# Token loads in pairs, query weights on ScalarE's queue, and two blocks' statistics moved, in the opening of a transformer layer on one core

## The chip, the cores and the metric

The kernel runs on one core of a Trainium2 chip. The metric is the device time of one execution in microseconds (us), as the median of several runs. A profiled execution gives the trace from which durations come; its span runs from its first to its last instruction.

The engines go by these names in the views: PE is TensorE's matmul and PEld its weight load, DVE is VectorE, ACT is ScalarE, POOL is GpSimd, SP is SyncE, which here only issues DMA transfers. Each engine runs its own instructions in order and waits for others on semaphores.

## The reference

One layer over 2048 tokens of width 640, in bf16: layer norm, attention with a compressive memory over four segments of 512 tokens and 32 heads of 20, a residual, a second layer norm, and a two-layer block with 1728 hidden units. Cut to what bears on the opening:

```
q = (layernorm(x) @ wq)   k = (layernorm(x) @ wk)   v = (layernorm(x) @ wv)
for s in range(4):
    p = softmax(qs @ ks^T * scale + mask)
    o = g * (phi(qs) @ M / (phi(qs) @ z)) + (1 - g) * (p @ vs)
    M += phi(ks)^T @ vs;  z += sum(phi(ks))
h  = x + o @ wo
h2 = h + silu(layernorm(h) @ w1) @ w2
```

The layer norm needs, for each token, mean and variance over 640 elements, and then `(x - mean) * (var + eps) ** -0.5`.

## The kernel before

Tokens are handled in blocks of 128 (one token per partition), four blocks to a segment; the block index is b. Weights stay in SBUF. The program is a graph of named tasks, and a hand-kept list, `ORDER` (L382), says in which order the tasks are emitted. Each engine's instruction stream is that list filtered for the engine; a suffix picks the engine where a task may run on two (`/D` VectorE, `/A` ScalarE, `/G` GpSimd), and numbers after a colon are buffer slots. A tracker turns reads and writes into semaphore waits, so a task waits only where it stands in its own engine's stream; what is behind it on that engine waits too.

The steps of the opening, for the first segment:

- `load_x` (L595, issued in L598) loads token blocks. Before, block 0 (`x0`), block 1 (`x1`) and blocks 2 and 3 together (`x2`) are three loads on SyncE.
- `load_w` (L600, issued in L601) loads weights. The query and key weights come in two pieces each (`w_q0`, `w_q1`, `w_k0`, `w_k1`: 3 and 2 of the 5 chunks of 128 rows) into the raw buffer `wraw`, then the value weights (`w_wv`) and `beta`. All are on SyncE, in this order. Blocks 4 to 11 (`x4`, `x8`) follow; they wait for the first piece of the key weights.
- `zpad` (L616) is a block of zeros made by VectorE. `warm` (L618) is one ScalarE activation of Tanh on it, whose output is overwritten later; a load of the activation table goes with it.
- `fillN` are N matmuls of zeros on TensorE (L637), which compute nothing.
- `n1_st` is a block's statistics. On VectorE (L785 to L791): two half-row statistics, their merge and, for the blocks called early, the addition of eps. On ScalarE (L778, L780): two activations with a running sum, which give the sum and the variance, and later `n1_mn` (L801), which gives the mean. Before, blocks 0, 1 and 3 are on VectorE and block 2 is on ScalarE.
- `n1_rs` is the reciprocal root on GpSimd: one power (L808) for early blocks, an addition and a power (L811, L813) for the others.
- `n1_ap` (L819) on VectorE applies mean and root. `n1_tp` (L828) transposes a block on TensorE by five matmuls with the identity, and `n1_te` copies the result out of PSUM, on ScalarE (L837) or VectorE (L838).
- `pr00` are the first projections, from the raw weights (L752): x and y are the first and the second half of the segment's tokens (blocks 0 and 1, blocks 2 and 3), the digit before them is 0 for queries and 1 for keys, and .0 and .1 are the two pieces of the weights. There are 80 matmuls in all. `re_wq` and `re_wk` (L745, L747) reorder the weights for the later projections.
- `mq0` and `mq1` (L703) are small masks on GpSimd, needed much later.

The order of the opening before (buffer slots left out), as far as the prediction walks it:

```
VectorE: zpad sel st0 st1 ap0 st3 ap1 ap3 ap2 te3 ...
ScalarE: warm st2 te0 mn2 te1 re_wq1 te2 ...
TensorE: fill25 fill4 fill8 tp0 tp1 fill2 tp3 pr000x.0 tp2 pr000x.1 pr001x.0 pr001x.1 pr001y pr000y ...
```

Of the kernel before, what the change touches and what calls it, by code (L numbers as in the profile page):

```python
# [11 lines left out]
PE, AC, DV, PO, SP = "pe", "act", "dve", "pool", "sp"  # L12
# [333 lines left out]
D = 640  # L346
# [26 lines left out]
KS = [range(0, 3), range(3, 5)]  # L373
# [7 lines left out]

ORDER = """  # L382
x0:0 zpad:0 iota fill25:7 vpad0 x1:3 sel halfc mq0 x2:5,6 warm:0 w_q0:0 epsc w_q1 n1_st0:1 w_k0:0 w_k1 w_wv:0 n1_st1:0
n1_rs0 beta n1_ap0:0 n1_rs1 fill4:5 n1_st2:5,1 n1_st3:4 fill8:5 mq1 n1_tp0:2 n1_ap1:2 n1_rs3 n1_te0:1 n1_tp1:0 n1_rs2
fill2:5 n1_ap3:3 n1_mn2 n1_te1 n1_tp3:6 n1_ap2 re_wq1/A:0 pr000x.0:3 n1_te3/D x4:2,10,11,1 n1_tp2:4 pr000x.1
x8:9,8,4,7 n1_te2 pr001x.0:1 qe000x/D:0 re_wk1/G pr001x.1 re_wk2/A pr001y.0:2 re_wk4/G pr001y.1 qe001x pr000y.0:6
qe001y pr000y.1 re_wk3/G pr010.0/C:0 pa001:2 qe000y ex001:1 re_wq2/G qk0a0:4,1 lsc0 pr010.1 e0a2:0 lsc1 pr011.0:7
qe010/D:0 e0a0 pr011.1 qk0b0:0,2 qe011/D pr020.0/C:6 e0b2:3 mk0a pb001 pr020.1/C re_wk0/G n1_st4:3 e0b0 qk0e0:2,4
pr021.0:7 re_wq4/G e0e0:5 n1_st5:1 v00.0:0 vpad2 n1_rs4 e0e2 v00.1 qe020/D:0 pr021.1 n1_rs5 n1_st10:7 ve00:0 qk1a0:2,4
# [94 lines left out]
def build(nc, es, A_x, A_wq, A_wk, A_wv, A_wo, A_beta, B_x, B_w1, B_w2, out):  # L484
    T = Tracker()
# [9 lines left out]
    G = Graph(pools)  # L495
# [7 lines left out]
    wv_sb = sb("wv_sb", [128, NC, D], BF16)  # L503
# [65 lines left out]
    def R(*items):  # L569
        r = []  # L570
        for a, subs in items:
            r += a.keys(subs)
        return r

    def dma(name, reads, writes, fn, prio, bw, kind="plain", lane=None, engs=(SP,)):
        ln = T.lane(name) if lane is None else lane

        def emit(eng):
            T.add(eng, lambda e: fn(e), reads=R(*reads), writes=R(*writes), lane=ln)
        cost = {"tr": 1.31, "plain": 0.47, "sb": 0.72, "fix": 0.47}[kind]  # L580
        t = G.task(name, {e: cost for e in engs}, emit, reads, writes, prio, mode=kind, bw=bw)
        return t
# [5 lines left out]
    W = {k: G.alloc(k) for k in ("wq", "wk", "wv", "wo", "w1", "w2")}  # L588
    C = G.alloc("const")
# [3 lines left out]
    sT0 = G.alloc("sT")  # L593

    def load_x(b0, n, prio, bw=2.1, kind="plain", engs=(SP, AC)):  # L595
        s0 = b0 % 12
        dma(f"x{b0}", [(W["wk"], ["p"])] if b0 >= 4 else [], [(X[b], [0]) for b in range(b0, b0 + n)],
            lambda e: e.dma_start(out=x_tok[:, s0:s0 + n, :], in_=xv[:, b0:b0 + n, :]), prio, bw, kind, engs=engs)  # L598

    def load_w(k, dst, src, prio, bw, wr, kind="plain", engs=(SP, AC)):  # L600
        dma("w_" + k, [(W["wk"], ["p"])] if kind == "plain" else [], wr, lambda e: e.dma_start(out=dst, in_=src), prio, bw, kind, engs=engs)  # L601

    cw = lambda w: w.rearrange("(c p) e -> p c e", p=128)
    load_x(0, 1, -100, 2.30, "fix", (SP,))
    load_x(1, 1, -99, 2.33, "fix", (SP,))
    load_w("wv", wv_sb[:, :, :], cw(A_wv), -98, 4.96, [(W["wv"], [0])], "fix", (SP,))
    load_x(2, 2, -97, 4.79, "fix", (SP,))
    dma("beta", [], [(C, ["beta_bc"])],
        lambda e: e.dma_start(out=beta_bc[:, :],
                              in_=A_beta.rearrange("(o n) -> o n", o=1).to_broadcast([128, H])), -92, 4.65, "fix")  # L610
    for w_, (n_, src) in enumerate((("q", A_wq), ("k", A_wk))):
        for z, ks in enumerate(KS):
            k0_, k1_ = ks[0], ks[-1] + 1
            load_w(f"{n_}{z}", wraw[:, w_, k0_:k1_, :], cw(src)[:, k0_:k1_, :], -94 + w_, 6.58, [(sT0, [f"{n_}{z}"])] + ([(W["wk"], ["p"])] if n_ + str(z) == "k0" else []), "fix",
                   (SP,))
    G.task("zpad", {DV: 0.3}, lambda e_: T.add(DV, lambda e: e.memset(zpad[:, :], 0.0), writes=R((C, ["zpad"]))),  # L616
           [], [(C, ["zpad"])], -101)
    G.task("warm", {AC: 1.15}, lambda e_: T.add(AC, lambda e: e.activation(  # L618
        out=w2_sb[:, NF - 1:NF + 1, :], in_=zpad[:, 0:1].unsqueeze(2).to_broadcast([128, 2, D]), func=ACT.Tanh),
        reads=R((C, ["zpad"])), writes=R((W["w2"], [4, 5]))), [(C, ["zpad"])], [(W["w2"], [4, 5])], -100)  # L620
# [28 lines left out]
    def vpad(par, vt, wr=()):  # L649
# [8 lines left out]
        writes=["iota"], prio=-70)  # L658
    cst("sel", DV, 0.12, lambda e: e.tensor_scalar(out=ident[:, :], in0=iot[:, :], scalar1=0.0, scalar2=None,
                                                   op0=ALU.is_equal), reads=["iota"], writes=["sel"], prio=-70)  # L660
    sel = ident[:, :].rearrange("p (r e) -> p r e", e=32)[:, :, 0:VS]
# [5 lines left out]
        out=bsel[:, :], in_=bsel[:, :], pattern=[[0, NG], [-32, 4]], compare_op=ALU.is_equal, fill=0.0, base=-DH,  # L667
        channel_multiplier=1), reads=["bsel"], writes=["bsel"], prio=-1)
    cst("lsc2", DV, 0.25, lambda e: e.tensor_reduce(
        out=lsc[:, :], in_=bsel[:, :].rearrange("p (g r) -> p g r", r=4), axis=mybir.AxisListType.X, op=ALU.add),  # L670
# [95 lines left out]
    def layer_norm(tag, b, xa, xsub, dstA, i, prio):  # L766
# [5 lines left out]
        def e_stats(eng):  # L772
# [17 lines left out]
            if early:  # L790
                T.add(DV, lambda e: e.tensor_scalar(out=mvt[:, s, 1:2], in0=mvt[:, s, 1:2], scalar1=EPS, scalar2=None,  # L791
                                                    op0=ALU.add),
                      reads=R((st, ["mv"])), writes=R((st, ["mv"])))
        early = tag == "n1_" and b in (0, 1, 3)
        onact = tag == "n1_" and b == 2
        G.task(f"{tag}st{b}", {AC: 1.6} if onact else {DV: 1.03}, e_stats, [(xa, xsub)],
               [(st, ["s0", "mv"] if onact else ["s0", "s1", "mv"])] + ([(xn, [0])] if onact else []), prio)
        if onact:
# [55 lines left out]
    def declare_front(s):  # L854
# [5 lines left out]
        for i in range(4):  # L860
            layer_norm("n1_", 4 * s + i, X[4 * s + i], [0], xTa, i, k0 + P["ln1"] + P["ln1s"] * i if s else -30 + i)
# [531 lines left out]
```

## Time and profile before

| | us |
|---|---|
| median of 3 runs | 292.81 (292.77 to 293.06) |
| the profiled execution | 292.8 |
| its span | 291.1 |

The profile's page gives, for each engine, its busy time and its share of the span. The chain of waits is followed back from the last instruction: each piece is the work, or the transfer, that the next piece waited for. The timeline lists instructions in order of time, with start and duration in us, neighbours of one kind merged, and in brackets how long the engine had been idle before them and who ended that. A table by stretches of time gives each engine's busy time, then the granted TensorE clock (PEclk), the mean busy share of the 16 DMA engines, and the GB/s that they moved. The list of DMA issues gives, for each kind of load, how many there were, the size of one and the median time from its issue to its landing, when the last byte is there and its waiter may go on.

### The profile page before, as it was taken

The numbers are of one execution on the slowest core, as the hardware profiler recorded it, in microseconds if no ns is written. First come the engines' busy times: TensorE is split into PE (matmuls) and PEld (weight loads), VectorE is DVE, ScalarE is ACT, GpSimd is POOL, SyncE is SP. The second block draws the span as 40 slices with busy tenths as digits, with TensorE's granted clock in tenths as the row PEclk, the third lists the DMA queues.
The fourth block names the chain that finished last, engine by engine and source line by source line (L and its number), as shares of the span: only waits on it lengthen the run. The fifth ranks groups of instructions, "written<-read, shape, count | busy, mean of one in ns | idle before, by whom it ended". The sixth has DMA issues, their size and how long they took to land.

```text
span 291.1 us, 10526 instructions
## 1 busy us (share of the span) xinstructions
PE 283.0 (97%) x4587; PEld 156.9 (54%) x4587; DVE 208.7 (72%) x435; ACT 224.7 (77%) x286; POOL 138.1 (47%) x275
## 2 busy tenths in 40 slices
PE   8999989999999999999999999999999999999995
PEld 6544434445544446566643554655565557754674
DVE  5599889769998679369979972776676659436513
ACT  4999999999999999999689989999849750024300
POOL 4686668608670766609516761638435531200000
PEclk9999999999999999999999999999999999999999
DMA  7916439854565333343551327512110031340004
GB/s 207 350 57 125 85 65 303 116 55 79 121 110 126 67 86 101 47 76 60 101 183 17 66 43 102 78 19 49 25 25 2 2 69 26 75 131 0 3 5 160
DMA packets 48734, 24.86 MB, mean 85 GB/s; under 512 B 38896, under 2 KB 47472, under 8 KB 48688
## 3 DMA queue, kind: packets, MB, share of 16 engines
q1 hardware_dynamic: 48688, 24.19, 37.9%
q8 instruction: 36, 0.59, 0.9%
q14 instruction: 10, 0.08, 0.1%
HBM read 10.41 MB, written 2.62 MB: 45 GB/s over the span
## 4 chain that ended last, share of the span: by engine, by line
PE 79%; ACT 13%; DVE 4%; DMA 2%; POOL 1%; issue 1%; SPq 0%; DVEq 0%; ACTq 0%
PE ps_all L565 41%; PE ps_all L566 23%; ACT PT L1024 9%; PE ps_all L1003 7%; PE ps_all L1059 5%; ACT PT L1020 2%; DMA x_tok<-in_A_x_dram 2%; PE ps_all L1130 1%; PE ps_all L752 1%; PE ps_all L1268 1%; ACT ex L930 1%; POOL PT L1036 1%; DVE om L1149 1%; ACT oTs L1073 1%; PE ps_all L1189 1%
## 5 line engine op out<-in xcount | busy, mean ns | idle before, releaser
L1024 ACT ACTIVATE PT<-ps_all 128x1024 bf16<-128x1024 f32 x122 | 117.9, 1030 | 7.9 <-PE ps_all L1003 6.8
L1036 POOL TENSOR_SCALAR_AFFINE_SELECT PT<-PT 128x512 bf16<-128x512 bf16 x128 | 81.6, 666 | 71.6 <-ACT PT L1024 59.5
L1281 ACT ACTIVATE th<-ps_all 128x512 f32<-128x512 f32 (+1 forms) x56 | 31.5, 591 | 30.1 <-PE ps_all L565 22.5
L1287 DVE SCALAR_TENSOR_TENSOR sT<-th,ps_all 128x512 bf16<-128x512 f32 (+1 forms) x56 | 36.2, 661 | 16.8 <-ACT th L1281 16.5
L1020 ACT ACTIVATE PT<-ps_all 128x2048 bf16<-128x2048 f32 x19 | 35.7, 1878 | 3.5 <-PE ps_all L1003 3.4
L565 PE MATMUL ps_all<-w_sb,sT 128*128 128x320 bf16 x252 | 37.0, 299 | 0.0
L565 PE MATMUL ps_all<-tT,w_sb 128*128 128x512 bf16 x151 | 36.4, 380 | 0.0
L1324 DVE SCALAR_TENSOR_TENSOR x_tok<-ps_all,x_tok 128x640 bf16<-128x640 f32 (+1 forms) x17 | 13.2, 782 | 24.5 <-PE ps_all L566 16.1
L565 PEld LDWEIGHTS ps_all<-w_sb,sT 128*128 128x128 bf16 x252 | 23.7, 98 | 11.0 <-issue 1.7
L566 PE MATMUL ps_all<-w_sb,sT 128*32 128x320 bf16 x784 | 28.8, 299 | 0.0
L785 DVE BATCH_NORM_STATS2 stt<-x_tok 128x6 f32<-128x320 bf16 x62 | 27.0, 478 | 2.0 <-DMA x_tok<-in_A_x_dram 1.9
L566 PE MATMUL ps_all<-tT,w_sb 128*32 128x512 bf16 x436 | 27.1, 380 | 0.0
L566 PEld LDWEIGHTS ps_all<-w_sb,sT 128*32 128x32 bf16 x784 | 20.1, 97 | 6.7 <-issue 0.9
L565 PEld LDWEIGHTS ps_all<-tT,w_sb 128*128 128x128 bf16 x151 | 13.6, 98 | 16.1 <-issue 1.9
L1111 POOL TENSOR_TENSOR otok<-otok,om 128x320 bf16<-128x320 bf16 x24 | 18.2, 781 | 4.2 <-DVE otok L1098 4.2
L565 PE MATMUL ps_all<-wv_sb,tT 128*128 128x320 bf16 x130 | 19.9, 300 | 0.2 <-DVE zf L677 0.2
L811 POOL TENSOR_TENSOR rst<-mvt,eps_c 128x1 f32<-128x1 f32 x29 | 5.8, 201 | 27.4 <-DVE mvt L788 27.4
L819 DVE TENSOR_SCALAR xn_rot<-x_tok,mvt,rst 128x640 bf16<-128x640 bf16 x32 | 16.7, 533 | 2.5 <-POOL rst L813 1.3
L813 POOL TENSOR_TENSOR rst<-rst,eps_c 128x1 f32<-128x1 f32 x29 | 16.4, 567 | 2.3
L1246 DVE TENSOR_TENSOR x_tok<-ps_all,x_tok 128x640 bf16<-128x640 f32 x16 | 13.0, 812 | 6.0 <-PE ps_all L565 6.0
L1059 PE MATMUL ps_all<-PT,Vx 128*32 128x512 bf16 (+3 forms) x384 | 16.9, 300 | 0.2 <-ACT PT L1024 0.2
L1098 DVE TENSOR_TENSOR otok<-ps_all,rd 128x320 bf16<-128x320 f32 x32 | 15.7, 491 | 1.1
(116 smaller groups left out, 427.8 us busy)
## 6 DMA issues: line engine op xcount, KB each, us to landing
out_dram<-x_tok SPq DMA_DIRECT2D x15, 160.0 KB, 2.0
w_sb<-in_B_w_dram SPq DMA_DIRECT2D x5, 432.0 KB, 4.6
x_tok<-in_A_x_dram SPq DMA_DIRECT2D x3, 640.0 KB, 5.1
w_sb<-in_B_w_dram SPq DMA_DIRECT2D x3, 480.0 KB, 4.1
QKV<-QK SPq DMA_DIRECT2D x12, 72.0 KB
wv_sb<-in_A_wv_dram SPq DMA_DIRECT2D x1, 800.0 KB, 8.9
wo_sb<-in_A_wo_dram SPq DMA_DIRECT2D x1, 800.0 KB, 4.8
w_sb<-in_B_w_dram SPq DMA_DIRECT2D x1, 640.0 KB, 4.7
```

The source lines that it names most:

```text
L565: return [lambda e: e.matmul(out, lhsT=lhsT, rhs=rhs, start=start, stop=stop)]
L566: return [lambda e, p=p: e.matmul(out[p:p + 32, :], lhsT=lhsT[:, p:p + 32], rhs=rhs, start=start, stop=stop, tile_position=(0, p)) for p i ...
L785: T.add(DV, lambda e, hh=hh: e.bn_stats(out=stt[:, s, 6 * hh:6 * hh + 6], in_=xb[:, 320 * hh:320 * hh + 320]), reads=R((xa, xsub)), writes ...
L819: T.add(eng, lambda e: e.tensor_scalar(out=xn_rot[:, xn.slot, :], in0=x_tok[:, b % 12, :], scalar1=mvt[:, s, 0:1], scalar2=rst[:, s, :], o ...
L1003: fns.append(lambda e, j=j, o=o, r=r, q0=q0, q1=q1, qa=qa, ka=ka: e.matmul(ps_all[:, o:o + q1 - q0], lhsT=ka[32 * r:32 * r + DH, 128 * j:1 ...
L1020: T.add(AC, lambda e: e.activation(out=o, in_=src, func=ACT.Exp, scale=SCALE), reads=[("ps", z.slot + q) for z in (a, b) for q in range(2) ...
L1024: T.add(AC, lambda e: e.activation(out=pt[:, pta.slot, q0:q0 + 2, 0:width], in_=sc3[:, b0:b0 + 2, 0:width], func=ACT.Exp, scale=SCALE), re ...
L1036: fns.append(lambda e, v=v: e.affine_select(out=v, in_=v, pattern=[[0, 4], [1, 128]], compare_op=ALU.is_ge, fill=0.0, base=0, channel_mult ...
L1059: fns.append(lambda e, j=j, r=r, h=h, pa=pa, pt=pt, co=co, q0=q0, ji=ji: e.matmul(bank(po)[32 * r:32 * r + 32, q0:hi], lhsT=vtile(vx)[:, j ...
L1111: T.add(PO, lambda e: e.tensor_tensor(out=o_dst, in0=o_dst, in1=m, op=ALU.add), reads=R((oma, WH), *osub), writes=R(*osub))
L1281: T.add(AC, lambda e: e.activation(out=th[:, tha.slot, lo:hi], in_=bank(ps)[:, lo:hi], func=ACT.Tanh, scale=0.5), reads=R((ps, [0])), writ ...
L1287: T.add(DV, lambda e: e.scalar_tensor_tensor(out=sT[:, f, lo:hi], in0=th[:, tha.slot, lo:hi], scalar=1.0, in1=bank(ps)[:, lo:hi], op0=ALU. ...
```

## The change

Four things change; all of them lie in the first row of `ORDER` and the declarations behind it.

1. Blocks 0 and 1 are one load (`x0`), as blocks 2 and 3 are. SyncE issues `x0`, `x2`, `w_k0`, `w_k1`, `w_wv`, `beta`, in this order.
2. `w_q0` and `w_q1` are issued by ScalarE. They are declared as reading `zpad`, so the first of them waits for the zero block. They stand ahead of `warm` on ScalarE.
3. The statistics of blocks 1 and 3 are on ScalarE, and those of block 2 on VectorE. Accordingly the early blocks, with one power on GpSimd, are 0 and 2, and there are `mn1` and `mn3` on ScalarE in place of `mn2`.
4. The first row of the order is rewritten up to `pr001x.0`, and is the old one from there on. On VectorE: st0 st2 ap0 ap1 ap2 te0 ap3 te3. On ScalarE: w_q0 w_q1 warm st1 mn1 st3 mn3 te1 te2 re_wq1. On GpSimd: rs0 rs1 mq1 rs2 rs3. On TensorE: fill25 fill4 tp0 fill8 tp1 tp2 fill2 pr000x.0 pr000x.1 tp3 pr001x.0. The copy of block 0 out of PSUM goes from ScalarE to VectorE.

```diff
 ORDER = """
-x0:0 zpad:0 iota fill25:7 vpad0 x1:3 sel halfc mq0 x2:5,6 warm:0 w_q0:0 epsc w_q1 n1_st0:1 w_k0:0 w_k1 w_wv:0 n1_st1:0
-n1_rs0 beta n1_ap0:0 n1_rs1 fill4:5 n1_st2:5,1 n1_st3:4 fill8:5 mq1 n1_tp0:2 n1_ap1:2 n1_rs3 n1_te0:1 n1_tp1:0 n1_rs2
-fill2:5 n1_ap3:3 n1_mn2 n1_te1 n1_tp3:6 n1_ap2 re_wq1/A:0 pr000x.0:3 n1_te3/D x4:2,10,11,1 n1_tp2:4 pr000x.1
-x8:9,8,4,7 n1_te2 pr001x.0:1 qe000x/D:0 re_wk1/G pr001x.1 re_wk2/A pr001y.0:2 re_wk4/G pr001y.1 qe001x pr000y.0:6
+x0:0,3 zpad:0 iota w_q0:0 w_q1 fill25:7 vpad0 sel halfc mq0 x2:5,6 warm:0 epsc w_k0:0 w_k1 w_wv:0 beta n1_st0:1 n1_st1:0,2 n1_rs0 n1_st2:5 fill4:5 n1_ap0:0 n1_rs1 mq1 n1_mn1 n1_tp0:2 n1_ap1 fill8:5 n1_tp1:0 n1_rs2 n1_st3:4,3 n1_ap2:1 n1_mn3 n1_rs3 n1_te0/D:1 n1_te1/A n1_tp2:4 n1_ap3 n1_te2 fill2:5 pr000x.0:3 pr000x.1 re_wq1/A:0 n1_tp3:6 n1_te3/D x4:2,10,11,1 x8:9,8,4,7 pr001x.0:1 qe000x/D:0 re_wk1/G pr001x.1 re_wk2/A pr001y.0:2 re_wk4/G pr001y.1 qe001x pr000y.0:6
...
-    load_x(0, 1, -100, 2.30, "fix", (SP,))
-    load_x(1, 1, -99, 2.33, "fix", (SP,))
-    load_w("wv", wv_sb[:, :, :], cw(A_wv), -98, 4.96, [(W["wv"], [0])], "fix", (SP,))
-    load_x(2, 2, -97, 4.79, "fix", (SP,))
...
+    load_x(0, 2, -100, 2.80, "fix", (SP,))
+    load_x(2, 2, -97, 3.40, "fix", (SP,))
+    for w_, (n_, src) in enumerate((("q", A_wq), ("k", A_wk))):
+        for z, ks in enumerate(KS):
+            k0_, k1_ = ks[0], ks[-1] + 1
+            dma(f"w_{n_}{z}", [(C, ["zpad"])] * (n_ == "q"), [(sT0, [f"{n_}{z}"])] + [(W["wk"], ["p"])] * (n_ + str(z) == "k0"),
+                lambda e, w_=w_, k0_=k0_, k1_=k1_, src=src: e.dma_start(out=wraw[:, w_, k0_:k1_, :], in_=cw(src)[:, k0_:k1_, :]),
+                -94 + w_, 5, "fix", engs=((AC, SP)[w_],))
+    load_w("wv", wv_sb[:, :, :], cw(A_wv), -90, 4.96, [(W["wv"], [0])], "fix", (SP,))
...
-        early = tag == "n1_" and b in (0, 1, 3)
-        onact = tag == "n1_" and b == 2
+        early = tag == "n1_" and b in (0, 2)
+        onact = tag == "n1_" and b in (1, 3)
```

The numbers in these declarations (priorities and costs) are not used when the order is written out by hand.

More of the change, by code (lines that the diff above doesn't have):

```diff
@@ L603, in build @@
     cw = lambda w: w.rearrange("(c p) e -> p c e", p=128)
-    load_x(0, 1, -100, 2.30, "fix", (SP,))
-    load_x(1, 1, -99, 2.33, "fix", (SP,))
-    load_w("wv", wv_sb[:, :, :], cw(A_wv), -98, 4.96, [(W["wv"], [0])], "fix", (SP,))
-    load_x(2, 2, -97, 4.79, "fix", (SP,))
+    G.task("zpad", {DV: 0.3}, lambda e_: T.add(DV, lambda e: e.memset(zpad[:, :], 0.0), writes=R((C, ["zpad"]))),
+           [], [(C, ["zpad"])], -101)
+    load_x(0, 2, -100, 2.80, "fix", (SP,))
[7 more added lines that the diff above has]
+    load_w("wv", wv_sb[:, :, :], cw(A_wv), -90, 4.96, [(W["wv"], [0])], "fix", (SP,))
     dma("beta", [], [(C, ["beta_bc"])],
@@ L610, in build @@
                               in_=A_beta.rearrange("(o n) -> o n", o=1).to_broadcast([128, H])), -92, 4.65, "fix")
[L611 to L617, printed above, removed]
     G.task("warm", {AC: 1.15}, lambda e_: T.add(AC, lambda e: e.activation(
```

## The prediction

> **What bounds the kernel now.** I read the page first, for what fills the span, and then the chain of waits in the first 14 us, because the diff touches only the loads and the first row of the written order.
>
> ```profile
> span 291.1 us, 10526 instructions
> PE 283.0 (97%) x4587; PEld 156.9 (54%) x4587; DVE 208.7 (72%) x435; ACT 224.7 (77%) x286; POOL 138.1 (47%) x275
> PE 79%; ACT 13%; DVE 4%; DMA 2%; POOL 1%; issue 1%; SPq 0%; DVEq 0%; ACTq 0%
> ```
>
> TensorE is busy all through, and the chain that ended last is TensorE with some ScalarE. So what the opening gains or loses should reach the end nearly whole: nothing behind it has room to give it back. The opening itself, from the chain restricted to 0 to 14 us (start, us, what):
>
> ```profile
> 1.72 4.91 DMA x_tok<-in_A_x_dram
> ...
> 6.65 0.90 DVE stt L785 x2
> 7.57 0.22 DVE mvt L788
> 7.82 0.16 DVE mvt L791
> 8.06 0.69 POOL rst L808
> 8.85 0.46 DVE xn_rot L819
> ...
> 9.80 0.47 PE ps_all L752 x12
> 10.31 0.45 PE ps_all L828 x5
> 10.77 2.07 PE ps_all L752 x68
> ```
>
> The reader sees that blocks 2 and 3 of the tokens, one load issued at 1.72, land at 6.63, and that statistics, root, apply, transposes and first projections (L752) follow without a gap. The opening is a race between the landing of blocks 2 and 3 and the steps behind it. The mark I use is the start of the second token half's projections (pr001y), when block 2 has been copied out of PSUM:
>
> ```profile
> 11.56 0.99 PEld L752 LDWEIGHTS ps_all<-tT,sT 128*32 128x32 bf16 x40 [0.20 <-ACT tT L837]
> ```
>
> From that task on the written order is the old one, so the change of the whole time is the change of this 11.56.
>
> **When the tokens land.** Issues and landings by load, and what the DMA moved (last column GB/s):
>
> ```profile
> x_tok<-in_A_x_dram SPq DMA_DIRECT2D x2, 160.0 KB, 2.3
> x_tok<-in_A_x_dram SPq DMA_DIRECT2D x1, 320.0 KB, 4.9
> sT<-in_A_wq_dram SPq DMA_DIRECT2D x1, 320.0 KB, 6.1
> sT<-in_A_wk_dram SPq DMA_DIRECT2D x1, 320.0 KB, 7.3
> ```
>
> ```profile
> 0.00:2.00 2.00, 0.88 (x5) 0.63 (x6) 0.89 (x2) 1.20 (x1) 1.23 (x10) 1.00 0.08 10
> 2.00:4.00 2.00, 2.00 (x11) 1.44 (x10) 0.89 (x2) 1.35 (x2) 0.55 (x5) 1.00 0.86 223
> 4.00:6.00 2.00, 2.00 (x11) 1.38 (x10) 1.87 (x7) 0.00 (x0) 0.84 (x2) 1.00 1.01 338
> 6.00:8.00 2.00, 2.00 (x20) 1.68 (x18) 1.28 (x5) 1.32 (x3) 0.98 (x5) 1.00 1.00 301
> ```
>
> ```profile
> 0.80 1.28 ACT L618 ACT_TABLE_LOAD   x1 [0.80 <-PEq L1378]
> 0.80 1.35 SPq L598 DMA_DIRECT2D x_tok<-in_A_x_dram  x3
> 0.90 0.17 DVE L616 MEMSET zpad<- 128x128 uint32 x1 [0.90 <-PEq L1378]
> 1.12 6.62 PE L637 MATMUL ps_all<-zpad 128*128 128x256 bf16 x37 [1.12 <-DVE zpad L616]
> 2.09 1.27 ACT L618 ACTIVATE w_sb<-zpad 128x1280 bf16<-128x1280 bf16 x1
> 2.20 1.00 SPq L601 DMA_DIRECT2D sT<-in_A_wq_dram  x2
> ...
> 3.10 0.89 DVE L785 BATCH_NORM_STATS2 stt<-x_tok 128x6 f32<-128x320 bf16 x2 [1.20 <-DMA x_tok<-in_A_x_dram]
> 3.24 1.00 SPq L601 DMA_DIRECT2D sT<-in_A_wk_dram  x2
> ...
> ...
> 4.26 0.15 DVE L791 TENSOR_SCALAR mvt<-mvt 128x1 f32<-128x1 f32 x1
> ...
> 6.37 0.61 POOL L703 TENSOR_SCALAR_AFFINE_SELECT mq<-mq 128x4 f32<-128x4 f32 x4
> 6.65 0.74 ACT L778 ACTIVATE xn_rot<-x_tok 128x640 bf16<-128x640 bf16 x1 [3.29 <-DMA x_tok<-in_A_x_dram]
> ...
> 8.25 0.19 ACT L780 ACTIVATION_READ_ACCUMULATOR xn_rot<-x_tok,stt 128x1 f32 x1
> 8.70 0.18 POOL L811 TENSOR_TENSOR rst<-mvt,eps_c 128x1 f32<-128x1 f32 x1
> 8.93 0.19 ACT L801 ACTIVATE mvt<-stt 128x1 f32<-128x1 f32 x1
> 8.97 0.73 POOL L813 TENSOR_TENSOR rst<-rst,eps_c 128x1 f32<-128x1 f32 x1
> 9.02 0.69 ACT L837 ACTIVATE tT<-ps_all 128x640 bf16<-128x640 f32 x1
> ...
> 10.17 0.82 DVE L838 CAST tT<-ps_all 128x640 bf16<-128x640 f32 x1
> ```
>
> The four token blocks are 655 kB (640 KB). By the rates, 20 + 446 kB had moved at 4.0, so 655 kB had moved at 4 + 189/338 = 4.56; yet the load landed at 6.63, when 1.33 MB had moved. Twice the tokens' bytes went by first: the 16 DMA engines don't finish a load together, and the last one was 2.07 us behind the mean. For block 0 (164 kB moved at 2.65, landed 3.08) that lag was 0.43. I have the lag from these two rows only, so I carry 0.43 and 2.07 as its bounds.
>
> After the change the load of blocks 2 and 3 is SyncE's second, at 1.26 in place of 1.72: 0.46 earlier. Against that, the query weights (640 x 640 in bf16, 819 kB) leave ScalarE's queue from about 1.1, the end of the zero block (0.90 + 0.17) in place of 2.20, and they are no longer behind these tokens. No row of before shows two loaded queues at once, so I bound it. If the queues didn't disturb each other, the landing is 4.56 - 0.46 + 0.43 = 4.5 with the small lag and 6.63 - 0.46 = 6.2 with the large one. If all query weights went first, it is the landing of the second query load, issued half way in its row at 2.70 and landing 6.1 later at 8.8, less 0.46: 8.3. With an even share from when both run, some 0.56 MB of weights pass with the tokens, 1.22 MB in all; that mean passes at 6 + 78/301 = 6.26, less 0.46 = 5.8, and with the lag 6.2 to 7.9. I take 6.9, between these two, because the DMA share is 1.0 from 4 us on: there is no idle rate for a second queue to use. For blocks 0 and 1, 328 kB with some 200 kB of weights, the same sum gives about 4.2 (bounds 3.3 to 5.0).
>
> The Trainium skill, page "DMA: Bandwidth & Descriptors", section "Issuing engines are not separate DMA queues", says that loads issued by different engines run on the same 16 DMA engines and interleave, and that issuing from several saves only the issuing time. That rule speaks against this change: by it alone the gain is an issue or two of SyncE's time, and the even share above is what remains; the share of 1.0 in the rows agrees, but no run here shows two queues yet.
>
> **The steps, one after the other.** ScalarE waits for the zero block at 1.07, issues two loads, and everything it has is behind them: table load, warm-up, then statistics. A SyncE weight issue takes 1.00/2 = 0.50; at that price ScalarE is free at 2.1, the table load (1.28) ends at 3.4 and the warm-up (1.27) at 4.7, against 3.36 before. (Bounds: free issues 3.4, issues twice as long 5.7.) Nothing needed the warm-up's output; but block 1's statistics now stand behind it. One block's statistics on ScalarE take 6.65 to 8.44 = 1.79, and then 0.19 for the mean: block 1 from 4.7 to 6.5, the mean to 6.7, block 3 from the landing, 6.9, to 8.7.
>
> VectorE loses two blocks' statistics (3.10 to 4.41 = 1.31 each) and gains block 2's; but the new order puts block 2's statistics *ahead of* block 0's apply. Block 0's are done at 5.5 and its root near 6.2, and then VectorE stands waiting for blocks 2 and 3: statistics 6.9 to 8.2, applies of 0, 1, 2 (0.46 each, all roots ready; that of block 2 takes 0.69 beside the first two) to 9.6, block 0's copy (now on VectorE, 0.82) to 10.4, apply of 3 to 10.9. GpSimd's roots of 1 and 3 become two instructions (0.18 and 0.73, with the gap 1.00 from 8.70 to 9.70): 6.6 to 7.6, then the mask rows (0.61) to 8.3, root of 2 to 9.0, of 3 to 10.0; none is last here.
>
> On TensorE 29 fillers stand ahead of block 0's transpose in place of 37 (37 took 6.62, so these end by about 6.5) and eight stand behind it. By the rate of the later fillers,
>
> ```profile
> 6.00:7.50 1.50, 1.50 (x15) 1.32 (x13) 1.00 0.99 284
> ```
>
> 0.10 each, those eight take 0.8. Transpose of 0 at 8.8, fillers 9.1 to 9.9, transpose of 1 to 10.35, copy of 1 on ScalarE (0.69) to 11.1, of 2 to 11.8. First projections (20 of the 80 matmuls that took 0.47 + 2.07 in the chain, 2.54/4 = 0.63) 11.1 to 11.75, transpose of 3 to 12.2, its copy on VectorE (0.82) to 13.05, and the second half starts at 13.1. That is 13.1 - 11.56 = **1.5 us later**.
>
> The key weights: 2.29 MB had to move for them before and after, and the last of them, issued half way in its row, landed at 3.74 + 7.3 = 11.0; issued earlier, they are there by 11, ahead of the 12.0 at which they are first used: no cost, and none while the shift is above -0.5. The value weights, beta and blocks 4 to 11 are issued behind them on SyncE and used later still: nothing. Sum: the profiled execution took 292.8 for a span of 291.1, and the median is 292.81, so the same 1.7 lie around the span: 292.8 + 1.5 = **294.3**. By the landing's bounds (the mark follows the landing one for one, at landing + 6.2): 7.9 gives +2.5, 6.2 gives +0.8. A measurement of this kernel tells some 0.2%, 0.6 us, from no change.
>
> **Rivals.**
> *The tokens come early and ScalarE's issues are cheap* (not slower). Landing at 5.0 or sooner, VectorE doesn't wait. Then ScalarE's warm-up is the bound: at 4.7 block 1's root ends at 7.6, the mask rows at 8.2, root of 2 at 8.8, apply of 2 and copy of 0 at 10.1, and the mark is 12.05, +0.5. With free issues all that is up to 1.3 sooner, and the key weights at 11.0 hold the mark: -0.5, 292.3. It decides when the landing is below 5.3. For it: the DMA's rate from 2 to 4 us is 223, not 338. Against: the lag.
> *The table load stays ahead of the two loads.* Then the change doesn't start the query weights early: issued from 2.1 (0.80 + 1.28), as before. Tokens are disturbed from 3.1 on only, landing about 6.4, warm-up done at 4.4: +0.9, 293.7. For it: the table load ran at 0.80, before the zero block that its instruction waits for.
> *TensorE's clock falls back.* Between 6.5 and 8.8 TensorE has nothing.
>
> ```profile
> L637 PE MATMUL ps_all<-zpad x39: 272/421/421, 1.1 to 8.8; 128*128 128x256 bf16 x39
> ```
>
> The first fillers took 421 ns and the later ones 272, at twice the pace, though the granted clock reads 1.00. Back in the slow pace, the eight fillers, first projections and two transposes cost 0.8 + 0.6 + 0.4 more, and the second half 1.0: +4.3, 297.1. The Trainium skill, "TensorE: Matmul & The Clock Gate", section "Part 1: The HAM clock gate", has half rate back after an idle window of about 3.4 us; the 2.3 us here are less, which speaks against it.
>
> **How the numbers follow.** Forecast (shared queues, landing 6.2 to 7.9) 0.5: 293.6 to 295.3, all slower. Early tokens 0.25: 292.3 to 293.3, of which 0.1 goes to faster by over 0.6 (it takes a little more than I worked out) and 0.15 to same. Table load first 0.15: 0.10 slower, 0.05 same. Clock 0.10: slower. Faster 0.10, same 0.20, slower 0.70. The range leaves out the clock and the very end of the early case: 292.2 to 296.0, its upper end from a landing at 8.3 (+2.9) and slow ScalarE issues.
>
> **What would show it.** Right: blocks 2 and 3 landing after 6.2; VectorE idle between block 0's statistics and block 2's; the transpose of block 0 after 8, the mark after 12.3. The warm-up ending near 4.7 shows the price of ScalarE's issues and the place of the table load; the fillers behind the first transpose at 272 or 421 ns show the clock. Wrong: a landing below 5.3, or a mark that moves while the end doesn't.

## The result and the profile after

The kernel after takes 294.71 us (294.54 to 295.37), the kernel before 292.79 (292.38 to 293.06); the ratio is 1.0071, with a 95% interval of 1.0051 to 1.0091. The profiled execution took 294.56, with a span of 292.8, 1.7 longer than before. The forecast of 294.3 was right in sign and size, but two of its terms were wrong and cancelled, as the rows show: that it came so close is luck.

First the chain of waits of after, from 0 to 15 us (start, us, what):

```profile
1.33 4.86 DMA x_tok<-in_A_x_dram
...
6.21 0.90 DVE stt L782 x2
...
7.45 0.45 DVE xn_rot L816
...
7.94 0.45 PE ps_all L825 x5
8.40 0.87 PE ps_all L634 x8
...
10.19 0.71 ACT tT L834
...
10.94 0.39 PE ps_all L634 x2
11.33 0.66 PE ps_all L749 x20
...
12.41 0.84 DVE tT L835
...
13.29 1.28 PE ps_all L749 x40
```

Blocks 2 and 3 now land at 6.19 (6.63 before), 4.86 after their issue. The mark, the second half's projections (L749 here), is at 13.29 instead of 11.56: 1.73 later, and the span is 1.7 longer. So the opening's delay reaches the end whole. From the landing to the mark it takes 7.10, where before it took 4.93. So against before the loss lies in the steps behind the landing, and the runs below have to show how early the tokens could have landed. The pair of lines at 10.94 and 11.33 was not in my walk: two fillers (L634) run only once ScalarE has copied block 2, and the first projections stand behind them.

The timeline shows ScalarE's part, VectorE's wait for the tokens, and these two fillers (the brackets give the idle time before the line and who ended it):

```profile
1.10 0.97 ACTq L609 DMA_DIRECT2D sT<-in_A_wq_dram  x2
...
2.10 1.28 ACT L615 ACT_TABLE_LOAD   x1 [2.10 <-issue]
...
3.39 1.27 ACT L615 ACTIVATE w_sb<-zpad 128x1280 bf16<-128x1280 bf16 x1
...
6.21 0.89 DVE L782 BATCH_NORM_STATS2 stt<-x_tok 128x6 f32<-128x320 bf16 x2 [1.06 <-DMA x_tok<-in_A_x_dram]
...
7.20 0.73 POOL L700 TENSOR_SCALAR_AFFINE_SELECT mq<-mq 128x4 f32<-128x4 f32 x4
...
8.76 0.45 DVE L816 TENSOR_SCALAR xn_rot<-x_tok,mvt,rst 128x640 bf16<-128x640 bf16 x1 [0.51 <-POOL rst L805]
...
10.94 0.39 PE L634 MATMUL ps_all<-zpad 128*128 128x256 bf16 x2 [1.11 <-ACT tT L834]
```

`fill2:5` writes PSUM bank 5. The slot of block 2's transpose, `tp2:4`, is the pair of banks 4 and 5, so the two fillers wait until block 2 is copied out. In before the same fillers stood behind the transpose of block 1, where that bank was free.

What the DMA moved, by stretches of 2 us (the last two columns are DMA share and GB/s):

```profile
2.00:4.00 2.00, 2.00 (x11) 1.44 (x10) 0.17 (x1) 1.89 (x2) 0.56 (x5) 1.00 0.95 310
4.00:6.00 2.00, 2.00 (x11) 1.38 (x10) 1.08 (x4) 1.97 (x4) 0.56 (x1) 1.00 1.05 377
6.00:8.00 2.00, 1.11 (x8) 0.68 (x7) 1.72 (x6) 1.97 (x7) 1.51 (x7) 1.00 1.07 368
```

The rates are 310, 377 and 368, where before had 223, 338 and 301. The first rise is not the second queue's: the runs below that have the token pairs and all weights on SyncE (e2, e4, e5, e7) show 298 to 315 there. From 4 to 6 us they show 270 to 296, so in that stretch the two queues of after moved more bytes; in e11 and e12, where the second queue's first packets came only after 4 us, it was 230 and 245. In after, the bytes that came early were the query weights. The list of transfers from 3 to 4 us, by queue (packets, MB, share; q10 is ScalarE's queue, q1 SyncE's), shows it:

```profile
q10 hardware_dynamic: 235, 0.30, 80.8%
q1 hardware_dynamic: 83, 0.09, 25.2%
```

From 2 to 3 us all packets were SyncE's (blocks 0 and 1). Then, although blocks 2 and 3 had been issued at 1.33, four fifths of the DMA's time went to the first query load, issued at 1.10.

### The profile page after: what moved, and what is told of

Its sections match the earlier page's. It is cut to its first block, busy times and chain, and to the rows that moved or that the text cites. A ratio compares the mean times of both kernels' runs of the same rounds, so it can differ in the third digit from the quotient of the medians.

```text
span 292.8 us, 10528 instructions
## 1 busy us (share of the span) xinstructions
PE 283.3 (97%) x4587; PEld 157.0 (54%) x4587; DVE 208.0 (71%) x432; ACT 226.1 (77%) x290; POOL 138.8 (47%) x276
## 4 chain that ended last, share of the span: by engine, by line
PE 79%; ACT 13%; DVE 4%; DMA 2%; POOL 1%; issue 1%; SPq 0%; ACTq 0%
PE ps_all L562 41%; PE ps_all L563 23%; ACT PT L1021 9%; PE ps_all L1000 7%; PE ps_all L1056 5%; ACT PT L1017 2%; DMA x_tok<-in_A_x_dram 2%; PE ps_all L1127 1%; PE ps_all L1265 1%; ACT ex L927 1%; POOL PT L1033 1%; PE ps_all L749 1%; DVE om L1146 1%; ACT oTs L1070 1%; PE ps_all L1186 1%
## 5 line engine op out<-in xcount | busy, mean ns | idle before, releaser
L782 DVE BATCH_NORM_STATS2 stt<-x_tok 128x6 f32<-128x320 bf16 x60 | 26.2, 478 | 3.2 <-DMA x_tok<-in_A_x_dram 3.0
L810 POOL TENSOR_TENSOR rst<-rst,eps_c 128x1 f32<-128x1 f32 x30 | 17.0, 568 | 2.3
```

The costliest lines, as they stand in the source:

```text
L782: T.add(DV, lambda e, hh=hh: e.bn_stats(out=stt[:, s, 6 * hh:6 * hh + 6], in_=xb[:, 320 * hh:320 * hh + 320]), reads=R((xa, xsub)), writes ...
L810: T.add(PO, lambda e: e.tensor_tensor(out=rst[:, s, :], in0=rst[:, s, :], in1=eps_c[:, 1:2], op=ALU.pow), reads=R((st, ["r"]), (C, ["half" ...
```

## The experiments

My theory at the start had two parts: the tokens land late because the query weights, issued before them, go ahead of them (**the queue**), and the two fillers hold the projections (**the bank**). Rivals: the new places of the statistics and copies make the opening late whatever the DMA does (**the order**), and TensorE falls back to a low clock (**the clock**). The runs are called e1 to e12 in the order in which they were made; the letters of theories in an expectation hold for that expectation. Each time is a median, beside that of the kernel before on the same chip. Unless another base is named, a diff is against the kernel after.

### e1: the fillers in another bank

```diff
 ORDER = """
...
-fill2:5
+fill2:7
...
```

> The changed kernel with one number changed: its last two fillers write PSUM bank 7 in place of bank 5, half of block 2's transpose. Theory (the fillers wait for ScalarE to copy block 2 out of that bank, and the first projections stand behind them): the first projections start at about 10.3 in place of 11.26, the second half's at about 12.3 in place of 13.29, and the time falls by some 0.9 us, to 293.8. Rival (the order on VectorE behind the token landing sets the mark alone): second half at 13.1 or later, time 294.5 to 294.7. Both: blocks 2 and 3 land at 6.2 as before this edit.

Measured: 294.35 against 292.80, ratio 1.0056 [1.0036, 1.0077]. The profiled execution showed something else. TensorE from 8 us on (timeline), and the granted clock by stretches (the third number from the end):

```profile
8.78 0.71 PE L825 MATMUL ps_all<-ident,xn_rot 128*128 128x128 bf16 x5 [2.25 <-DVE xn_rot L816]
9.28 1.91 PE L634 MATMUL ps_all<-zpad 128*128 128x256 bf16 x8
```

```profile
8.00:10.00 2.00, 1.22 (x9) 1.04 (x10) 1.81 (x6) 0.92 (x3) 1.47 (x3) 0.70 1.08 367
10.00:12.00 2.00, 2.00 (x16) 1.69 (x15) 0.94 (x2) 0.23 (x1) 2.00 (x6) 0.50 1.08 352
```

The tokens landed at 7.02 in this execution, TensorE had nothing for 2.25 us, and the clock fell to 0.50: eight fillers took 1.91 instead of 1.04. So the price of the bank can't be read from this execution. It is one of two, out of ten, in which the mean granted clock of the whole execution was 0.994. In the other eight it was 0.999 or 1.000, and their median is 294.17: 1.37 above before, against 1.92 for after, so the bank is worth about 0.5, where 0.9 was expected. The clock rival is real, though not in after, where the wait was 0.89 in the profiled execution and all four executions had 0.999 or 1.000.

### e2 and e7: the query loads back on SyncE, then the other bank as well

```diff
-            dma(f"w_{n_}{z}", [(C, ["zpad"])] * (n_ == "q"), [(sT0, [f"{n_}{z}"])] + [(W["wk"], ["p"])] * (n_ + str(z) == "k0"),
+            dma(f"w_{n_}{z}", [], [(sT0, [f"{n_}{z}"])] + [(W["wk"], ["p"])] * (n_ + str(z) == "k0"),
...
-                -94 + w_, 5, "fix", engs=((AC, SP)[w_],))
+                -94 + w_, 5, "fix", engs=(SP,))
```

In the order they stand behind `x2` and `warm`. The second kernel, e7, also has `fill2:7`.

> The changed kernel with the query weights back on SyncE, behind both token loads, and not waiting for the zero block; all else as changed. Theory (the two queues take turns by whole transfers, so the first query piece, 0.49 MB, goes between the token loads): blocks 2 and 3 land by 5.0 in place of 6.2; ScalarE's warm-up ends at 3.4; second half's projections at about 12.4, time 293.7. Rival (the landing is 4.9 us after its issue whatever shares the engines, as in both traces so far): landing 6.1 to 6.2, second half at 13.0 or later, time 294.4.

Measured: 293.82 against 292.80, 1.0030 [1.0017, 1.0043].

> The run with the query weights on SyncE, with the last two fillers in bank 7 in place of bank 5. Theory (those fillers wait for block 2's copy, and the first projections behind them): first projections start at 9.1 in place of 10.06; the key weights, landing at 11.2, and block 3's copy then set the second half, 11.3 in place of 12.09; time 293.1 in place of 293.8. Rival (not those fillers): 12.0 and 293.8.

Measured: 292.99 against 292.96, 1.0000 [0.9988, 1.0011]. The chains of the two, the first with `fill2:5`, the second with `fill2:7`:

```profile
8.38 1.31 ACT tT L834 x2
...
9.74 0.39 PE ps_all L634 x2
10.13 0.66 PE ps_all L749 x20
...
12.09 1.27 PE ps_all L749 x40
```

```profile
9.29 0.73 PE ps_all L749 x20
...
11.41 1.28 PE ps_all L749 x40
```

One digit moves the projections from 10.13 to 9.29 and the mark from 12.09 to 11.41. With both undone, nothing is left of the loss: in sum, pairing the tokens, moving the statistics and the rest of the new order cost nothing that can be told. That is the end of the rival "order", by which the opening is late whatever the DMA does. It does not make the new order free. In e7 block 2's statistics start at 5.12, 1.53 sooner than before, but the mark stands 6.29 behind them instead of 4.91, so the new order uses up what the early landing gives. The loss is the two fillers and the move of the query loads.

### e8: the other bank with ScalarE's loads kept, and TensorE kept busy

```diff
 ORDER = """
...
-fill4:5
+fill12:5
...
-fill2:5
+fill2:7
...
```

> The changed kernel with the last two fillers in bank 7 and eight more fillers ahead of the first transpose (37 in place of 29, the number in the kernel before), so that TensorE has no gap of over 1.5 us before that transpose. Theory (in the run with the bank alone the granted clock fell to 0.5 from 8.6 to 12 us after a gap of 2.25 us, and took back what the bank gave): granted clock 1.00 in the profile, second half's projections at 12.3 to 12.6, time 293.6. Rival (the clock is not it): time 294.3 as with the bank alone, or the clock below 1 again.

Measured: 294.36 against 292.96, 1.0045 [1.0029, 1.0061]. With 37 fillers ahead of the first transpose the clock stayed at 1.00, but the time is the rival's 294.3 and not the 293.6 of the theory. The chain of waits:

```profile
1.10 0.42 ACTq L609
...
3.38 1.27 ACT w_sb L615
...
7.22 0.58 POOL mq L700 x4
7.80 0.63 POOL rst L805
...
12.64 1.28 PE ps_all L749 x40
```

The statistics of block 2 started at 6.34, so the mark stands 6.30 behind them. In after it is 13.29 - 6.21 = 7.08. The fillers therefore cost 0.8 of the mark here; measured the same way it is 0.8 in the last pair too (12.09 - 4.98 = 7.11 and 11.41 - 5.12 = 6.29). But this chain does not pass through the landing. It goes from ScalarE's two issues through the table load and the warm-up (ending at 4.65) to block 1's statistics, and then on GpSimd through block 1's root, the masks (7.22) and block 2's root (7.80). The variance of block 2 was ready at 7.66, so the path from the landing is only some 0.1 us shorter: with the fillers out of the way, tokens that land earlier would alone gain no more than that. In the medians' differences to before:

| | fillers wait for block 2 | they don't |
|---|---|---|
| query loads on SyncE | +1.02 | +0.03 |
| query loads on ScalarE | +1.92 (after) | +1.40 |

The kernel of +1.40 also has eight more fillers; e1 without them has +1.37 in its eight executions at full clock. The bank costs 0.5 to 1.0 and the move of the query loads, ScalarE's issues included, 0.9 to 1.4. With both the loss is less than the sum of the two alone (2.4). The mark moved by +1.08 in this last kernel and the median by 1.40. VectorE's last addition, the last piece of the chain, moved by 1.08 as well (before, then this kernel):

```profile
288.15 0.49 DVE x_tok L1324
289.23 0.49 DVE x_tok L1321
```

So all of the opening's shift arrives there, and what is left lies behind it, where only the last results go out: 2.5 us from the end of that piece to the end of the span in before, 3.1 in this kernel's profiled execution. Why that differs stays open.

### e4: the pair of tokens alone

This is before with blocks 0 and 1 in one load, the old statistics and the old order.

```diff
...
-    load_x(0, 1, -100, 2.30, "fix", (SP,))
-    load_x(1, 1, -99, 2.33, "fix", (SP,))
+    load_x(0, 2, -100, 2.80, "fix", (SP,))
```

> The kernel before with one part of the change: blocks 0 and 1 in one load, so that blocks 2 and 3 are issued 0.46 us earlier; all weights on SyncE, statistics and order as before. Theory: with nothing between the token loads and no rival queue, blocks 2 and 3 land by 5.0; rival (4.9 after the issue): 6.2. By both, block 0's statistics start 0.7 us later (3.8), VectorE is busy with blocks 0 and 1 until 6.9, so what the earlier landing gives is kept only in part: second half's projections 11.2 to 11.5, time 292.4 to 292.8.

Measured: 293.03 against 292.80, 1.0012 [0.9997, 1.0028]: no difference that can be told. The two token loads land a median of 3.3 after their issue, against 4.9 for blocks 2 and 3 before; ScalarE starts on block 2 at 4.79, when they have landed (6.65 before). But VectorE, which got block 0 later than before (3.90 instead of 3.10), had blocks 0 and 1 to do first and got to block 3 at 6.71 (6.65 before). Tokens that land early gain nothing while VectorE is the next bound.

### e3: the query loads on ScalarE alone

This is before with only `w_q0` and `w_q1` moved to ScalarE, ahead of `warm`.

```diff
 ORDER = """
-x0:0 zpad:0 iota fill25:7
+x0:0 zpad:0 iota w_q0:0 w_q1 fill25:7
...
```

> The kernel before with one part of the change: the query weights on ScalarE, behind the zero block and ahead of the warm-up; single loads of blocks 0 and 1, statistics and order as before. Theory (turns by whole transfers): blocks 0 and 1 go first, one query piece next, blocks 2 and 3 land at 6.0 to 6.3; ScalarE is free for block 2's statistics at 4.7, so nothing waits for the warm-up; second half's projections 11.1 to 11.3, time 292.4 to 292.6. Rival (landing 4.9 after the issue, at 6.6): 11.6 and 292.8.

Measured: 295.32 against 292.80, 1.0077 [1.0052, 1.0102]. I had expected the two queues to take turns, and a small gain; that theory fell here. The chain, and the clock:

```profile
1.73 6.38 DMA x_tok<-in_A_x_dram
...
8.14 0.90 DVE stt L786 x2
```

```profile
10.00:12.00 2.00, 1.67 (x24) 0.78 (x22) 1.15 (x3) 1.82 (x4) 1.92 (x5) 0.85 0.99 286
12.00:14.00 2.00, 1.90 (x31) 1.38 (x33) 1.20 (x3) 1.15 (x2) 2.00 (x7) 0.50 1.06 388
```

Here both query loads were issued before blocks 2 and 3 (1.73), and the tokens landed at 8.11: 1.5 later than with the queries behind them. That is close to the prediction's upper bound (8.3, all query weights first), in a kernel where both were issued first. TensorE then waited 2.21 us and its clock fell to 0.50. Four of the six executions had a mean granted clock of 0.994. The other two (0.998 and 1.000) took 294.64 and 294.27, so the late tokens cost 1.5 to 1.8 and the clock about 1 more.

### e6: the query loads behind the warm-up in ScalarE's order

```diff
 ORDER = """
-x0:0,3 zpad:0 iota w_q0:0 w_q1 fill25:7 vpad0 sel halfc mq0 x2:5,6 warm:0 epsc
+x0:0,3 zpad:0 iota fill25:7 vpad0 sel halfc mq0 x2:5,6 warm:0 w_q0:0 w_q1 epsc
...
```

> The changed kernel with the two query loads behind the warm-up on ScalarE in place of ahead of it, so that they are issued at about 3.4 in place of 1.1; still on ScalarE's queue, all else as changed. Theory (turns by whole transfers): when the first token load ends the other queue is still empty, so blocks 2 and 3 go next and land by 5.0; the query pieces take turns with the key pieces and are there by 9.2; ScalarE's statistics start at 4.4 to 4.6 as changed; second half's projections at 12.2 to 12.6, time 293.7. Rival (a second loaded queue costs the tokens their time whenever it starts, by sharing): landing 6.0 or later, second half at 13.0 or later, 294.5.

Measured: 295.01 against 292.96, 1.0076 [1.0053, 1.0098]. The place in the order did not delay the loads. ScalarE in the timeline:

```profile
0.80 1.28 ACT L615 ACT_TABLE_LOAD   x1 [0.80 <-PEq L1375]
...
1.11 0.96 ACTq L609 DMA_DIRECT2D sT<-in_A_wq_dram  x2
2.10 1.27 ACT L615 ACTIVATE w_sb<-zpad 128x1280 bf16<-128x1280 bf16 x1
```

They were issued at 1.11 during the table load, ahead of the warm-up that stands before them. The warm-up ended 1.3 sooner than in after, block 1's statistics began at 4.11 instead of 4.57, and the time was no better: the chain goes through the landing at 6.32, not through ScalarE.

### e9 and e12: the query loads held back until the tokens are issued

Two kernels hold ScalarE's loads back, by a read of block 0 (issued at 4.84) and by a read of VectorE's selector `sel` (issued at 1.93, behind the token loads at 0.80 and 1.33 and the first key load at 1.82).

```diff
-            dma(f"w_{n_}{z}", [(C, ["zpad"])] * (n_ == "q"), [(sT0, [f"{n_}{z}"])] + [(W["wk"], ["p"])] * (n_ + str(z) == "k0"),
+            dma(f"w_{n_}{z}", [(X[0], [0])] * (n_ == "q"), [(sT0, [f"{n_}{z}"])] + [(W["wk"], ["p"])] * (n_ + str(z) == "k0"),
```

In e9 the loads also stand behind `n1_st1` in the order. e12 is e6 with this in place of the zero block (`late`, new here, lists what the issue waits for besides):

```diff
-                -94 + w_, 5, "fix", engs=((AC, SP)[w_],))
+                -94 + w_, 5, "fix", engs=((AC, SP)[w_],), late=[(C, ["sel"])] * (n_ == "q"))
```

> The changed kernel with the two query loads still on ScalarE's queue but issued only once the first token load has landed (they stand behind block 1's statistics and read block 0), at about 3.8; the run with the loads behind the warm-up had not delayed them, because ScalarE issued them at 1.11 while the warm-up was still waiting to run. All else as changed, the filler bank too. Theory (turns by whole transfers): blocks 2 and 3 have their turn before the query weights are there and land at 4.5 to 5.0; second half's projections 12.0 to 12.4, time 293.6 to 293.9, as with the query weights on SyncE. Rival (a second queue takes from the tokens whenever it is used): landing 6.0 or later, 294.5 or more.

Measured: 299.44 against 292.81, 1.0219 [1.0196, 1.0242]. The tokens landed early (median 3.4 after issue), but the query loads landed 8.3 and 9.6 after theirs, at 13.1 and near 15. From 8 to 9 us the transfers of ScalarE's queue were still these, against 292 on SyncE's:

```profile
q10 hardware_dynamic: 4, 0.01, 1.4%
```

All that SyncE had issued before 4.84 (key and value weights, 1.6 MB) went first. So I made the theory sharper: transfers go in the order of issue, over both queues. e12 was to test that.

> The kernel of e6 with one thing changed: ScalarE's two query loads wait for VectorE's selector (ends at 1.90 us) in place of the zero block, so they are issued at about 1.95 instead of 1.10, behind the load of blocks 2 and 3 (1.33). Theory A (order of issue over both queues): blocks 2 and 3 land at 4.5 to 5.0 as when the query loads were on SyncE, in place of 6.2 to 6.3; the second half's projections start at about 12.1 to 12.4 in place of 13.3, and the time is 293.6 to 293.9. Theory B (a second loaded queue takes its share from the tokens, whatever was issued first): landing 6.0 to 6.3, the second half at 13.2 to 13.4, time 294.7 to 295.0.

Measured: 296.04 against 292.99, 1.0099 [1.0077, 1.0122]. The sharper theory was half right. The tokens did land early, by 1.33 + 3.8 = 5.1 (instead of 6.19 in after), as this row for the two token loads says:

```profile
DMA to landing us min/median/max: 3.1/3.4/3.8
```

But the query loads landed 9.2 and 10.4 after issue, and everything behind them was late:

```profile
11.29 0.51 PE L749 MATMUL ps_all<-tT,sT 128*32 128x256 bf16 x12 [0.80 <-DMA sT<-in_A_wq_dram]
12.79 0.12 PEld L749 LDWEIGHTS ps_all<-tT,sT 128*32 128x32 bf16 x8 [1.27 <-DMA sT<-in_A_wq_dram]
```

Strict order of issue would have had the second query load through by 10.0 us: the six loads issued up to it are 2.29 MB, and 2.51 MB had moved by then (2 us times 7, 291, 245, 325 and 387 GB/s). It landed at 12.75, later than even the large lag of before (2.07) would allow. The transfers by queue, from 7 to 8 us and from 11 to 12 us, show where it went:

```profile
q10 hardware_dynamic: 127, 0.16, 51.6%
q1 hardware_dynamic: 130, 0.16, 48.5%
...
q1 hardware_dynamic: 321, 0.31, 103.9%
q10 hardware_dynamic: 9, 0.01, 3.4%
```

From 6 to 9 us, when both are running, they share about evenly, and the last few packets of the query load come through one by one while SyncE's queue, which still holds key, value and token loads, takes the rest. So issue time decides who starts; then comes sharing; and the landing of the queue with little in it is its last packet. Late weights replaced late tokens.

### e5, e10 and e11: attempts at a faster kernel

All three have the token pairs, fillers off block 2's bank, three fillers in place of eight behind block 0's transpose, and an order of projections rewritten for early tokens. e5 has all loads on SyncE; its row of TensorE's order is cut here:

```diff
...
-                -94 + w_, 5, "fix", engs=((AC, SP)[w_],))
+                -94 + w_, 5, "fix", engs=(SP,))
```

> A version meant to be faster than both kernels: token pairs and all weights on SyncE as in the run with the query weights on SyncE, and the opening's order rewritten by what the traces show: fillers only in a bank that nobody waits for and never behind a copy, the masks behind the roots, block 0's and 2's copies on ScalarE, block 1's and 3's on VectorE, the second half's query projections ahead of the last key piece, four small copies moved between engines. Theory (turns, and waits written into the order): blocks 2 and 3 land at 4.5, block 3's copy ends by 10.5, the first projections end at about 12.0 in place of 12.84, time 291.9 to 292.2. Rival (the last key piece, landing near 11.2, holds everything): first projections end at 12.5 to 12.8, time 292.5 to 292.8.

Measured: 292.86 against 292.96, 0.9992 [0.9980, 1.0003]: no difference. The 80 projections end at 12.42 (12.84 before), but 48 of them start only at 10.93, when block 3 has been copied. The chains of the two kernels, laid side by side, show where the 0.42 goes: 0.30 is left at 16.98, 0.15 at 71.11, behind twelve us in which the chain of before is ScalarE's, and 0.13 at VectorE's last addition (288.02 against 288.15). A gain in the opening is given back in part where another engine sets the pace.

e10 has the query loads on SyncE and the key loads on ScalarE, held back by a read of block 0:

```diff
-                -94 + w_, 5, "fix", engs=((AC, SP)[w_],))
+                -94 + w_, 5, "fix", engs=((SP, AC)[w_],))
```

> A version meant to be faster than both kernels: token pairs and query weights on SyncE, the two key loads on ScalarE's queue once the first token load has landed, and the opening's order as in the reordered SyncE run, with block 3's transpose ahead of the first projections and the key projections of the first half back ahead of the second half. Theory: tokens land at 4.5, the pieces take turns (queries, keys, queries, keys), all by 9.5 in place of 11.1, because two queues keep the DMA at 370 GB/s; block 3's copy ends by 10.5 and the 80 first projections by 12.0 in place of 12.84; time 291.9 to 292.3. Rival (what the opening gains is lost again later, as in the reordered SyncE run, whose projections ended 0.4 us earlier for 0.1 us of time): 292.6 to 292.9.

Measured: 296.32 against 292.81, 1.0100 [1.0074, 1.0127]. The key loads, issued at 4.71 behind 800 KB of value weights, landed at 12.5 and 13.4. Neither the theory nor the rival allowed for that.

e11 holds the key loads back by the selector alone:

```diff
-                -94 + w_, 5, "fix", engs=((SP, AC)[w_],))
+                -94 + w_, 5, "fix", engs=((SP, AC)[w_],), late=[(C, ["sel"])] * (n_ == "k"))
```

> Both token pairs, then both query pieces, the value weights and beta in SyncE's queue; both key pieces in ScalarE's, held back until VectorE's selector is written (1.90 us), so issued at about 1.95, behind the tokens' issues and level with the query pieces'. TensorE's order as in e10. Theory A (transfers go in the order in which they were issued, over both queues): tokens at 4.5 to 5.0, query pieces at about 6 and 8, key pieces at about 7.5 and 9.5; the 80 projections of the opening end at about 11.9 (12.84 before) and the time is 291.9 to 292.3. Theory B (a second loaded queue takes from the first, whatever was issued first): tokens at about 6, the first projections at 11 or later, and the time is 293.5 to 294.7. Theory C (what the opening gains is given back later because VectorE and ScalarE set the end of the opening's work): tokens early, but time 292.6 to 292.9.

Measured: 294.16 against 292.99, 1.0047 [1.0026, 1.0068]. That is the time of theory B, but not for its reason, as the two token loads landed a median of 3.4 after their issue. The chain:

```profile
2.33 9.19 DMA sT<-in_A_wq_dram
...
11.57 2.12 PE ps_all L752 x68
```

With the key loads in the other queue at the same time, the second query load took 9.2 to land; with all loads on SyncE (e5) it takes 6.4. Each share of the DMA given to the keys early was taken from the queries, which are needed first. No version beat the kernel before.

## Why the prediction was right, and where it was not

- **That the opening's shift is the whole shift: right** for after (mark +1.73, VectorE's last addition +1.85, span +1.7). In some experiments the time moved by 0.3 to 0.5 more than the mark, which the prediction didn't allow for; in e8 that lies behind the last addition.
- **Landing of blocks 2 and 3 at 6.9: too late by 0.7.** It was 6.19, inside the bounds, but just under the 6.2 at which the forecast's own band begins. The even share was not how it went: from 3 to 4 us the query load issued 0.23 earlier took 0.30 of 0.39 MB, and from 4 to 6 us the queues moved 0.42 and 0.34 MB. So by 6.0 some 0.72 MB of query weights had passed, where the prediction counted 0.56. The tokens still came sooner than forecast, because the rates were higher (the prediction's 1.22 MB had passed at 5.57, not at 5.8) and the landing was 0.62 behind that point, not 1.1. The argument that there was no idle rate was wrong: from 4 to 8 us the rates rose from 338 and 301 to 377 and 368. The large lag, 2.07, came from one row; with all loads on SyncE and the tokens in pairs (e4) the landing was 1.9 sooner than before, so it was no constant of a load.
- **ScalarE: right.** Two issues cost 0.97 (expected 1.00), the table load came behind them (2.10), the warm-up ended at 4.66 (expected 4.7). The rival in which the table load stays ahead and holds the loads back did not happen; even where the table load starts first (e6), the loads were issued at 1.11.
- **VectorE stands waiting, because block 2's statistics are ahead of block 0's apply: right**, 1.06 idle.
- **GpSimd "none is last here": right for the path only.** The mask rows (7.20) stood ahead of block 2's root, and VectorE waited 0.51 for it, but the chain goes through the fillers (8.40) to block 2's copy, not through that root. With the two fillers in another bank it does go through GpSimd: in e8 through block 1's root, the masks and block 2's root, which is the walk of the rival of early tokens (warm-up done at 4.7, masks to 8.2, root of 2 to 8.8; measured 4.65, 7.80 and 8.43).
- **The steps behind the landing, 6.2: too short by 0.9.** The walk let the first projections start when block 1 was copied (11.1), and passed over the two fillers ahead of them, which write block 2's bank and so wait for its copy (11.8). Both pairs of runs (e2 and e7, after and e8) price them at 0.8; with them out of the way the mark is 6.3 behind the landing, close to the 6.2, though in e8 the chain does not pass through the landing. So 0.7 too much and 0.9 too little made 13.1 out of a true 13.29.
- **The rival of early tokens** failed on its condition: the tokens came at 6.19, not below 5.3. Early tokens were not the whole condition either: where the loads made them early, the loss was still 1.0 with the fillers in the bank (e2) and 3.0 with the query loads behind the tokens on ScalarE (e12, with the clock's fall in it); it went to zero, not below, in e7.
- **The clock rival** did not happen in after: TensorE's wait was 0.89, not the 2.3 of the walk. It did in two of ten executions of the same kernel with one filler slot changed (e1), when the landing was 0.8 later. It cost about 1.7 there (295.78 and 296.04 against 294.17); the prediction had 2.8 for it.

## What to carry to other kernels

In these runs a load moved to a second queue took the DMA from loads issued after it on the first, needed sooner or not; look at issue times over all queues, and put what is needed first there first. In a written order, follow each dummy or filler instruction to the buffer it writes: it waits like any other, and what stands behind it waits too. A sum that comes out right can hide two errors, so compare each term, not the total.

## What was not expected of the hardware

- **Two queues are neither in order nor in turns.** For a load issued at 1.10, ScalarE's first packets came between 2 and 3 us behind block 0 alone (e3) and between 3 and 4 behind blocks 0 and 1 (after); they came between 4 and 5 for one issued at 1.93 behind three loads of SyncE (e12), and after 8 for one issued at 4.84 behind six (e9). In e12 the queues then shared about evenly (127 and 130 packets from 7 to 8 us); in after the first us went 235 to 83. The Trainium skill, "DMA: Bandwidth & Descriptors", section "Queues, rings and completion order", says that each DMA engine takes turns between the queues that it has work for, a packet at a time. The even phase agrees with that; the start by issue time does not follow from it. Why a later load starts so late was not settled.
- **The clock falls sooner than a long pause.** It fell to 0.50 in e1 at about 8.8, at the end of a wait of 2.25 us on TensorE, and in e3 at about 11.4, 1.5 us after a wait of 2.21 had ended. It held through one of 1.87 (e6), but in e9 it fell at about 12.2, 1.8 us into a wait of 2.98 (granted clock 0.54 from 12 to 14 us). These times are estimates from the mean clock of a stretch, with the fall as one step. So the length of the wait alone does not decide. The mean granted clock was 0.994 or less in 2 of 10 executions of e1, 4 of 6 of e3, 1 of 6 of e6, 5 of 5 of e9, 4 of 6 of e10, 3 of 12 of e11 and 3 of 6 of e12, and in none of the other kernels, so the medians of these seven hold a share of it. With the query loads behind the selector it fell (e12) without any wait of a matmul over 1.1 us, after six us of about half work (busy 1.02 of 2 us from 8 to 10, then these):

```profile
10.00:12.00 2.00, 0.90 (x14) 0.37 (x14) 0.00 (x0) 0.04 (x1) 0.92 (x2) 1.00 1.07 344
12.00:14.00 2.00, 1.21 (x29) 0.85 (x33) 0.38 (x1) 1.16 (x2) 2.00 (x7) 0.94 1.04 364
14.00:16.00 2.00, 2.00 (x44) 1.27 (x40) 0.77 (x2) 0.78 (x3) 0.32 (x1) 0.50 0.69 243
```

  The Trainium skill, "TensorE: Matmul & The Clock Gate", section "Part 1: The HAM clock gate", gives an idle window of about 3.4 us for the fall to half rate; the prediction used that against the clock rival, and the runs here don't bear it out.
- **A DMA issue on ScalarE passes an activation that stands before it** in the same order, if its own wait is over: issued at 1.11, with the warm-up ahead of it starting at 2.10.
